# Memory denominators of four head groups as one column-tiled quartet, with the reciprocals moved across partitions by copies

## Chip, cores and metric

One core of one Trainium2 chip. The metric is the device time of one execution in microseconds (us); lower is better. Kernels of one set of rounds ran in turn on the same chip; the sets of the experiments ran on three different chips, so across sets a kernel is best compared by its distance from the kernel before of its own set. An execution counts as fast when it is within 1.5% of the fastest of the same kernel. All times below are of fast executions unless it is said otherwise.

## The reference, cut to what matters

A transformer block: layer norm, an attention with a compressive memory over four segments of 512 tokens (32 heads of 32), output projection, then a gated feed-forward part. The change touches the memory's part of the attention:

```python
for s in range(N):                                   # N = 4 segments
    ...
    pq = phi(qs)
    num = jnp.einsum('bhld,bhde->bhle', pq, M)
    den = jnp.einsum('bhld,bhd->bhl', pq, z)[..., None] + 1e-06   # the memory denominator
    a_mem = num / den
    o = g * a_mem + (1.0 - g) * a_dot                # a_dot: softmax attention, with its own denominator
    ...
    M = M + jnp.einsum('bhld,bhle->bhde', pk, vs)
    z = z + jnp.einsum('bhld->bhd', pk)
```

In the first segment the kernel has no memory part, so the memory denominator is needed in three segments. A segment is worked on in two halves of four groups with four heads each: six half-segments with a memory.

## The kernel before, the parts that matter

Every operation is first recorded in a graph with a cost in ns. A planner then plays the graph through (a list scheduler with priorities), and the order in which each engine gets its instructions is fixed by that play. `SHIFT` is a table of small changes to the priorities, one entry per unit of work, found by a search for the shortest play. On the chip each engine has its list and waits on semaphores.

```python
def schedule(self):                       # the planner
    for o in ops:
        late, cls = SHIFT.get(o.unit, (0, 0))
        o.seq += late + 1e-6 * o.seq
        o.cls += cls
    ...
                    cost = o.cost[e]      # the planned duration decides what comes next
    ...
                    elif e == "dve" and o.port:
                        begin = max(begin, until["pool"])   # port=True: not planned to begin beside a GpSimd instruction
    ...

def finish(self, s, g0, at):              # one half-segment; g0: first of its four groups
    gd = self.queue(4)                    # PSUM bank 4: all denominators
    if s:                                 # memory denominators: 4 full matmuls, 128 columns of weights each
        self.mms(gd, [(lambda gr: self.bank(gr), self.zsel[:, g0 + i, :], self.pq[:, i, :],
                       i == 0, i == 3, 512) for i in range(4)], 2)
    ...
    column(gd, range(4), lambda i, kc, j: self.ones32[:, i, :], ...)   # softmax denominators, tiled 128*32
    ...                                   # column(...) for v: the numerators
    G.op("dve", ..., e.transpose(T1, self.bank(gr)))        # 32x32 blocks: tokens to partitions
    if s:
        ... tensor_scalar(td, td, 1e-6, None, op0=ALU.add)  # on the memory part
    ... reciprocal(rc, tr)                # both kinds at once, into Rc[p, group, kind, block]
    for n, i in enumerate(order):         # per group
        ...
        sp = ... transpose(dst, src)      # Rc back to R, spread over 32 partitions
        ...
        m = self.mms(gm, [(lambda gr: self.bank(gr), Mb, pq, True, True, 512)], 3)   # num
        G.dep(m, sp)                      # planned behind the transpose
        prev = ... scalar_tensor_tensor(R1, self.bank(gr), gcol, R1, ...)   # num * g / den
        ... tensor_tensor(oT, R0, R1, op=ALU.add)
```

The weights zsel of the full matmuls had their columns placed so that the memory denominator of group i, head j came out in partition strip j (32 partitions), next to the softmax denominator of the same head.

The softmax here doesn't subtract the row's maximum and nothing guards it: scores larger than these inputs give would overflow.

## Time and profile before

| | before |
|---|---|
| time, median of 6 executions | 904.32 us (903.87 to 904.83) |
| profiled span | 901.8 us |
| TensorE busy | 896.5 us, 99% |
| matmul engine's own waits | 2.5 us, all before 11 us |
| VectorE, ScalarE, GpSimd busy | 47%, 32%, 20% |

How to read it: the kernel is bound by TensorE's stream of matmuls, and the stream has no holes after the start. The prediction shows the lines. One more view, VectorE's timeline behind one denominator block (start us, length us, engine, line, operation):

```profile
128.25 0.72 DVE L1101 STREAM_TRANSPOSE T<-ps 128x512 f32<-128x512 f32 x1 [1.73 <-PE ps L1080]
...
130.27 0.94 DVE L1114 RECIPROCAL Rc<-T 128x128 f32<-128x128 f32 x1
131.13 0.36 DVE L982 TENSOR_TENSOR Macc<-Macc,ps 128x258 f32<-128x258 f32 x1
131.41 1.23 DVE L1134 STREAM_TRANSPOSE R<-Rc 128x1024 f32<-128x1024 f32 x1
```

The chain is: transpose T1, reciprocal, transposes into R. From the start of T to the first R are 3.16 us.

### The profile page before, as it was taken

The page shows a single profiled execution, that of the slowest core. Times are in us where ns is not written, and L with a number is a line of the kernel's source. Part 1 is how long each engine was busy: PE and PEld are TensorE (multiplying, and loading weights), DVE is VectorE, ACT ScalarE, POOL GpSimd, SP SyncE. Part 2 cuts the span into 40 slices and gives each one's busy share as a digit, 9 for nine tenths or more (in the row PEclk, how much of TensorE's full clock was granted, in tenths as well). Part 3 has the DMA queues.
Part 4 walks back from the last instruction along what each step waited for, and adds up shares of the span by engine and source line. Part 5 has one row for each costly group of instructions (what it writes and reads, how often), then busy time and mean ns, then how long its engine had stood idle before and what let it go on. Part 6 is the DMA issues. An engine that isn't in the chain of part 4 may idle for free.

```text
span 901.8 us, 13023 instructions
## 1 busy us (share of the span) xinstructions
PE 896.5 (99%) x5561; PEld 408.8 (45%) x5561; DVE 423.8 (47%) x653; ACT 286.0 (32%) x306; POOL 179.9 (20%) x243
## 2 busy tenths in 40 slices
PE   8999999999999999999999999999999999999998
PEld 5444444444434444444444444444444444444445
DVE  5683868878685766564434311201343334431111
ACT  6775867686675711111211100000111111110000
POOL 2554546467473422010000000000000000000000
PEclk9999999999999999999999999999999999999999
DMA  7879672545641268554322301013123221301110
GB/s 234 215 203 276 186 151 83 153 140 118 165 117 48 71 234 222 153 155 112 94 74 67 94 30 41 24 47 94 48 76 93 71 66 52 94 24 41 37 40 30
DMA packets 146473, 96.27 MB, mean 107 GB/s; under 512 B 45424, under 2 KB 133616, under 8 KB 146416
## 3 DMA queue, kind: packets, MB, share of 16 engines
q1 hardware_dynamic: 146416, 95.45, 38.5%
q8 instruction: 44, 0.72, 0.3%
q14 instruction: 13, 0.11, 0.0%
HBM read 76.55 MB, written 8.39 MB: 94 GB/s over the span
## 4 chain that ended last, share of the span: by engine, by line
PE 99%; DMA 1%; DVE 0%; SPq 0%; issue 0%
PE ps L701 92%; PE ps L1080 4%; PE ps L1035 3%; DMA xs<-in_A_x_dram 1%; PE ps L713 0%; SPq L292 0%; DVE lnst L827 0%; DVE xnT L725 0%; DVE ob L1229 0%; DVE xs L858 0%; DVE lnve L853 0%
## 5 line engine op out<-in xcount | busy, mean ns | idle before, releaser
L701 PE MATMUL ps<-hnT,w1b 128*128 128x512 bf16 x896 | 220.0, 379 | 0.0
L701 PE MATMUL ps<-hnT,w3b 128*128 128x512 bf16 x896 | 219.1, 379 | 0.0
L1197 ACT ACTIVATE sg<-ps 128x512 bf16<-128x512 f32 x112 | 66.9, 597 | 428.8 <-PE ps L701 428.8
L701 PE MATMUL ps<-w2b,hm 128*128 128x512 bf16 (+1 forms) x924 | 196.4, 373 | 0.0
L1200 DVE SCALAR_TENSOR_TENSOR t<-sg,ps 128x512 bf16<-128x512 bf16 x112 | 76.8, 686 | 192.2 <-ACT sg L1197 192.1
L1047 ACT ACTIVATE et<-ps 128x2048 bf16<-128x2048 f32 x80 | 149.9, 1874 | 29.1 <-PE ps L1035 28.8
L701 PEld LDWEIGHTS ps<-w2b,hm 128*128 128x128 bf16 x924 | 90.4, 98 | 103.3
L701 PEld LDWEIGHTS ps<-hnT,w1b 128*128 128x128 bf16 x896 | 87.1, 98 | 105.9 <-issue 7.6
L701 PEld LDWEIGHTS ps<-hnT,w3b 128*128 128x128 bf16 x896 | 87.2, 98 | 105.6 <-issue 1.0
L1056 POOL TENSOR_SCALAR_AFFINE_SELECT et<-et 128x512 bf16<-128x512 bf16 x96 | 85.3, 895 | 86.8 <-ACT et L1047 79.7
L1205 DVE SCALAR_TENSOR_TENSOR hm<-t,ps 128x512 bf16<-128x512 bf16 x112 | 76.8, 686 | 38.2 <-PE ps L701 35.5
L1229 DVE TENSOR_TENSOR ob<-hr,ps 128x512 bf16<-128x512 bf16 (+1 forms) x33 | 22.2, 671 | 143.0 <-PE ps L701 143.0
L701 PE MATMUL ps<-xnT,wp 128*128 128x512 bf16 (+1 forms) x352 | 62.1, 321 | 0.3 <-DVE lnve L853 0.2
L701 PE MATMUL ps<-wo,oT 128*128 128x512 bf16 x256 | 61.7, 379 | 0.0
L701 PE MATMUL ps<-hnT,wp 128*128 128x512 bf16 x256 | 61.5, 380 | 0.0
L701 PEld LDWEIGHTS ps<-xnT,wp 128*128 128x128 bf16 x352 | 27.6, 98 | 25.3 <-issue 3.5
L701 PEld LDWEIGHTS ps<-wo,oT 128*128 128x128 bf16 x256 | 24.4, 98 | 29.9 <-issue 1.7
L701 PEld LDWEIGHTS ps<-hnT,wp 128*128 128x128 bf16 x256 | 23.2, 98 | 28.7 <-issue 4.1
L1134 DVE STREAM_TRANSPOSE R<-Rc 128x1024 f32<-128x1024 f32 (+1 forms) x32 | 34.5, 1094 | 0.0
L1035 PE MATMUL ps<-qT,kT 32*128 32x128 bf16 (+3 forms) x512 | 31.7, 301 | 0.0
L701 PE MATMUL ps<-wp,hnT 128*128 128x512 bf16 x128 | 31.3, 380 | 0.0
L701 PE MATMUL ps<-wp,xnT 128*128 128x512 bf16 x128 | 31.0, 380 | 0.0
(85 smaller groups left out, 547.3 us busy)
## 6 DMA issues: line engine op xcount, KB each, us to landing
w3b<-in_B_w_dram SPq DMA_DIRECT2D x28, 512.0 KB, 3.9
w1b<-in_B_w_dram SPq DMA_DIRECT2D x28, 512.0 KB, 4.0
wp<-in_A_wv_dram SPq DMA_DIRECT2D x8, 1024.0 KB, 5.5
wp<-in_A_wq_dram SPq DMA_DIRECT2D x7, 1024.0 KB, 5.9
wp<-in_A_wk_dram SPq DMA_DIRECT2D x7, 1024.0 KB, 6.0
w2b<-in_B_w_dram SPq DMA_DIRECT2D x7, 1024.0 KB, 5.6
xs<-in_A_x_dram SPq DMA_DIRECT2D x16, 256.0 KB, 5.3
h<-in_A_x_dram SPq DMA_DIRECT2D x16, 256.0 KB, 3.3
```

Source lines behind the costliest of these rows:

```text
L701: return [e.matmul(p[0](gr), p[1], p[2], start=p[3], stop=p[4]) for p in part]
L1035: ins.append(e.matmul(self.bank(gr, j, 512 - 128 * kc, off), k[r, g0 + g, 128 * kc:128 * kc + 128], q[r, g0 + g, 128 * kc:512], start=True ...
L1047: return [e.activation(et[:, :, :], src, AF.Exp, scale=self.scale)]
L1056: self.pool_op(lambda e, v=v, pat=pat: e.affine_select(v, v, pattern=pat, compare_op=ALU.is_ge, fill=0.0, base=0, channel_multiplier=-1), ...
L1080: ins.append(e.matmul(self.ps[32 * j:32 * j + 32, b * 512 + 128 * kc:(b + 1) * 512], lhsT(i, kc, j), at[i, kc][:, j, :], start=kc == 0 and ...
L1134: sp = self.dve_op(lambda e, dst=dst, src=src: e.transpose(dst, src), dve_ns(512 * nr), [Rc[:, i, 0:nr, :]], [rs], 2)
L1197: self.g.op("act", act_ns(512), lambda e, gr, sg=sg: [e.activation(sg, self.bank(gr), AF.Tanh, scale=0.5)], writes=[sg], cls=0, group=gg)
L1200: e.scalar_tensor_tensor(t1, sg, 1.0, self.bank(gr), op0=ALU.add, op1=ALU.mult)], reads=[sg], writes=[t1], cls=0,
L1205: e.scalar_tensor_tensor(dst, t1, 0.5, self.bank(gr), op0=ALU.mult, op1=ALU.mult)], reads=[t1], writes=[dst], cls=0,
L1229: self.g.op("dve", dve_ns(n), lambda e, gr, hs=hs, ob=ob, n=n: [e.tensor_tensor(ob, hs, self.bank(gr, 0, n), op=ALU.add)], reads=[hs], wri ...
```

## The change

Intent: the four full matmuls use 128 columns of weights where 4 would do. As four column tiles (32 columns each, group i in partition strip i) they should run at once, for the price of one (217 ns by the spacing of the full matmuls before), as the quartets of the ones matmuls do in the trace before (136 ns for one of 320 columns in the mean, which is 320/512 of 217), and inside the operation that already runs tiled. The price: the denominator of group i, head j now comes out in strip i, and belongs in strip j. So the memory reciprocals go to a new tile Rm, and 16 small copies per half-segment carry them from strip to strip. The diff, without the table `SHIFT`, which is new in every entry:

```diff
@@ -605,7 +603,7 @@
         self.ocol = buf("ocol", [128, 8], F32)
         self.mhalf = buf("mhalf", [128, 1], F32)
         self.Mbf = buf("Mbf", [128, 8, 128], BF16)
-        self.zsel = buf("zsel", [128, 8, 128], BF16)
+        self.zsel = buf("zsel", [128, 8, 32], BF16)
         self.Macc = buf("Macc", [128, 8, 129], F32)
         self.lnst = buf("lnst", [128, 32, 12], F32)
         self.lnmv = buf("lnmv", [128, 32, 2], F32)
@@ -637,6 +635,7 @@
         r7 = at[0]
         self.et = [buf(f"et{i}", [128, 4, 512], BF16) for i in range(10)]
         self.Rc = buf("Rc", [128, 4, 2, 16], F32)
+        self.Rm = buf("Rm", [128, 4, 16], F32)
         self.R = [buf(f"R{i}", [128, 2, 512], F32) for i in range(2)]
 
         self.T1 = buf("T1", [128, 512], F32, self.g.base[self.R[1].name][1])
@@ -773,13 +772,13 @@
         o = self.ones32[:, :, :]
         P(lambda e: e.memset(o, 0.0), 128, [], [o], 1)
         for a in range(4):
-            oa = self.ones32[:, a, 2 * a:2 * a + 1]
+            oa = self.ones32[:, a, a:a + 1]
             P(lambda e, oa=oa: e.memset(oa, 1.0), 1, [], [oa], 1)
         for v in self.v:
             vo = v[:, :, :, 128:129]
             P(lambda e, vo=vo: e.memset(vo, 1.0), 32, [], [vo], 2)
         zz = self.zsel[:, :, :]
-        P(lambda e: e.memset(zz, 0.0), 1024, [], [zz], 3)
+        P(lambda e: e.memset(zz, 0.0), 256, [], [zz], 3)
         self.g.dma(self.beta[:, :], bass.AP(self.A_beta.tensor, self.A_beta.offset,
                                             [[0, 128], [1, 32]]), cls=3)
         gc, oc = self.gcol[:, :], self.ocol[:, :]
@@ -989,9 +988,7 @@
         self.either(lambda e, Mb=Mb, am=am, bl=bl: e.tensor_tensor(Mb, am, bl, op=ALU.mult),
                     256, 2, [am, self.blk[:, :]], [Mb], 4)
         for a in range(2):
-            col = 2 * (2 * pr % 4 + a) + 1
-            zs = self.zsel[:, 2 * pr + a, :].rearrange(
-                "p (j n) -> p j n", j=4)[:, :, col:col + 1].rearrange("p j n -> p (j n)")
+            zs = self.zsel[:, 2 * pr + a, 4:8]
             z = self.Macc[:, 2 * pr + a, 128:129]
             hm = self.hmask[:, :]
             self.pool_op(lambda e, zs=zs, z=z, hm=hm: e.tensor_scalar(
@@ -1060,20 +1057,23 @@
     def finish(self, s, g0, at):
 
 
+
         G = self.g
         G.stage()
         v = self.v[s % 2]
         gd = self.queue(4)
-        if s:
-            self.mms(gd, [(lambda gr: self.bank(gr), self.zsel[:, g0 + i, :], self.pq[:, i, :],
-                           i == 0, i == 3, 512) for i in range(4)], 2)
-
-        def column(gr, groups, lhsT, first, reads):
+
+        def column(gr, groups, lhsT, first, reads, zsel=None):
             G.stage()
 
             def emit(e, gr):
                 ins = []
                 b = gr.banks[0]
+                for i in range(4) if zsel else ():
+                    ins.append(e.matmul(
+                        self.ps[32 * i:32 * i + 32, b * 512:(b + 1) * 512],
+                        self.zsel[:, g0 + i, :], self.pq[:, i, :], start=True, stop=True,
+                        tile_position=(0, 32 * i), skip_group_check=True))
                 for i in groups:
                     for kc in range(4):
                         for j in range(4):
@@ -1084,12 +1084,14 @@
                                 tile_position=(0, 32 * j), skip_group_check=True))
                 return ins
 
-            o = self.mark = G.op("pe", len(groups) * (1280 / 2.4 + 12.0), emit,
-                     reads=[at[i, kc] for i in groups for kc in range(4)] + reads, cls=1, group=gr)
+            cost = len(groups) * (1280 / 2.4 + 12.0) + (216.0 if zsel else 0.0)
+            reads = (zsel or []) + [at[i, kc] for i in groups for kc in range(4)] + reads
+            o = self.mark = G.op("pe", cost, emit, reads=reads, cls=1, group=gr)
             o.mode = "col"
 
         column(gd, range(4), lambda i, kc, j: self.ones32[:, i, :], None if s else 0,
-               [self.ones32[:, :, :]])
+               [self.ones32[:, :, :]],
+               [self.zsel[:, g0:g0 + 4, :], self.pq[:, :, :]] if s else None)
         gn = {}
         order = (3, 0, 1, 2)
         for n, i in enumerate(order):
@@ -1101,17 +1103,20 @@
         G.op("dve", dve_ns(512), lambda e, gr: [e.transpose(T1, self.bank(gr))], writes=[T1],
              cls=0, group=gd)
         t1v = self.T1[:, :].rearrange("p (b r) -> p b r", r=32)
-        step = 1 if s else 2
         if s:
-            td = t1v[:, :, 1:8:2]
+            td = t1v[:, :, 4:8]
             self.dve_op(lambda e: e.tensor_scalar(td, td, 1e-6, None, op0=ALU.add), 217.0,
                         [td], [td], 0, port=True)
-            tr = t1v[:, :, 0:8]
-            rc = Rc[:, :, :, :].rearrange("p g t b -> p b (g t)")
-        else:
-            tr = t1v[:, :, 0:8:2]
-            rc = Rc[:, :, 0, :].rearrange("p g b -> p b g")
-        self.dve_op(lambda e: e.reciprocal(rc, tr), 150 + 6.2 * 128 / step, [tr], [rc], 0)
+        Rm = self.Rm
+        for n in range(2 if s else 1):
+            tr = t1v[:, :, 4 * n:4 * n + 4]
+            rc = Rm[:, :, :].rearrange("p j b -> p b j") if n else Rc[:, :, 0, :].rearrange(
+                "p g b -> p b g")
+            self.dve_op(lambda e, tr=tr, rc=rc: e.reciprocal(rc, tr), 150 + 6.2 * 64, [tr], [rc], 0)
+        for i in range(4 if s else 0):
+            for j in range(4):
+                a, b = Rc[32 * j:32 * j + 32, i, 1, :], Rm[32 * i:32 * i + 32, j, :]
+                self.dve_op(lambda e, a=a, b=b: e.tensor_copy(a, b), 90.0, [b], [a], 1)
         prev = None
         for n, i in enumerate(order):
             G.stage()
```

## The prediction

> **What bounds the kernel now.** I read the page's busy shares first, then its chain that ended last, then the table of waits for TensorE, then the timeline around the denominators, then the groups of instructions with shapes kept apart.
>
> ```profile
> PE 896.5 (99%) x5561; PEld 408.8 (45%) x5561; DVE 423.8 (47%) x653; ACT 286.0 (32%) x306; POOL 179.9 (20%) x243
> PE 99%; DMA 1%; DVE 0%; SPq 0%; issue 0%
> ```
>
> TensorE is busy for 896.5 of 901.8 us and 99% of the chain is matmuls. That busy time is a union of overlapping 379 ns records, so it could hide an array that is poorly fed. I therefore checked the waits of the matmul engine itself:
>
> ```profile
> PE ps L701 <- DVE oT L766: 1.2, 1, 1.2
> PE ps L713 <- DVE xs L858: 1.1, 2, 0.7
> PE ps L701 <- DVE lnve L853: 0.2, 1, 0.2
> ```
>
> These three lines are the whole answer, 2.5 us, and all lie in the first 11 us (warm-up and first layer norm). The weight-load row has a longer list, but its largest entries are "issue", in pieces of at most 0.5 us around changes of shape. So nothing that another engine does in the attention stages makes TensorE wait today. A change is worth what it takes out of TensorE's stream, provided it creates no wait that lasts.
>
> The stream around one half-segment's denominators (columns: start us, us, line, operation; x is the number of matmuls):
>
> ```profile
> 106.48 1.04 PE L701 MATMUL ps<-hnT,wp 128*128 128x512 bf16 x4
> 107.35 1.03 PE L701 MATMUL ps<-pq,zsel 128*128 128x512 bf16 x4
> 108.22 1.03 PE L701 MATMUL ps<-hnT,wp 128*128 128x512 bf16 x4
> ...
> 123.79 1.03 PE L701 MATMUL ps<-wo,oT 128*128 128x512 bf16 x4
> 124.75 1.27 PE L1080 MATMUL ps<-et,v 128*32 128x512 bf16 x32
> 125.85 2.35 PE L1080 MATMUL ps<-et,ones 128*32 128x512 bf16 x64
> 128.02 1.26 PE L1080 MATMUL ps<-et,v 128*32 128x512 bf16 x32
> 129.21 0.63 PE L701 MATMUL ps<-v,pkn 128*128 128x129 bf16 x8
> ```
>
> Starts matter here, not the printed lengths[...]. The four memory-denominator matmuls (moving pq, stationary zsel) occupy 108.22 - 107.35 = 0.87 us, or 217 ns each: full-array matmuls in a packed stream. The 64 column-tiled matmuls with the ones weights occupy 128.02 - 125.85 = 2.17 us. They are 16 quartets with widths 512, 384, 256 and 128, mean 320 columns, so a quartet costs 136 ns. If the four of a quartet ran one after another, 64 times 320/512 of 217 ns would be 8.7 us. Four column tiles therefore do run together, at the price of one matmul of their width. In all eight half-segments the column-tiled operations sit in one unbroken block of 128.
>
> [...] The quartets here reach about 4x (136 ns where a single 320-wide matmul would need 320/512 of 217 = 136 ns)[...]. [...] Here: the last full group starts at 123.79 and needs 0.87 us, to 124.66; the block starts at 124.75, so entry costs some 0.09 us. That price is already paid once per block. [...] TENSOR_SCALAR takes 149 ns for 128x1, 155 to 161 ns for 128x8 and 191 ns for 128x64.
>
> **The change, part by part.**
>
> TensorE, removed: 4 full matmuls per half-segment where there is a memory (segments 1 to 3, two halves each, so 6 times; the groups confirm 24 in all):
>
> ```profile
> L701 PE MATMUL ps<-pq,zsel 128*128 128x512 bf16 x24 | 6.2, 380 | 0.0
> L1080 PE MATMUL ps<-et,ones 128*32 128x512 bf16 x128 | 12.5, 379 | 0.0
> L1107 DVE TENSOR_SCALAR T<-T 128x64 f32<-128x64 f32 x6 | 1.1, 191 | 0.1
> L1114 DVE RECIPROCAL Rc<-T 128x128 f32<-128x128 f32 x6 | 5.7, 948 | 0.0
> L1114 DVE RECIPROCAL Rc<-T 128x64 f32<-128x64 f32 x2 | 1.1, 538 | 0.0
> ```
>
> TensorE, added: one quartet of 512 columns, emitted in the same operation as the ones matmuls, in the same tile shape (128*32). So no extra mode change, and by the quartet arithmetic it costs one matmul, 217 ns. Matmul and weight-load counts stay the same. Saving: 4 x 217 - 217 = 651 ns per half-segment, 6 x 651 ns = 3.9 us, all on the path that sets the end. If loading four 32-column weights ahead of the quartet exposed one weight load (97 ns in this trace), it would be 0.6 us less; the ones block shows no such gap, since its quartets already take what their columns need.
>
> VectorE: the reciprocal of 128x128 (948 ns) becomes two of 128x64 (538 each): +128 ns. The addition of 1e-6 stays 64 elements wide: 0. New: 16 copies of 32x16 f32 that move memory reciprocals from group i's partition strip to head j's. None is in the trace. A MEMSET takes 59 ns (32x1) and 85 ns (32x32), which puts 16 elements near 72 ns; the TENSOR_SCALAR times above, which read SBUF as the copies do, put 16 elements near 163 ns. I take 115 ns as an estimate between, so 1.8 us for 16 and about 2.0 us per half-segment with the reciprocals, 12 us over six. VectorE goes from 424 to about 436 us (431.5 to 440 with the two ends). These copies lie after the reciprocal and before the four block transposes into R, so the memory part of each half-segment (R, the Mbf matmul, oT) comes some 2 us later. That is off TensorE's path as long as TensorE has other work queued. It has: in the 13 us after the block at 124.75 it alternates hnT,wp, wo,oT and Mbf matmuls without a wait.
>
> GpSimd: clearing zsel falls from 1024 to 256 elements (1030 ns once, at 1.8 us). TensorE waits there for VectorE and input loads. Worth 0.
>
> Placement: the long table of shifts is new throughout, so all engines' orders are re-tuned. I can size only the room it has. TensorE waits just 2.5 us, all at the start, and the count of mode changes is fixed by 80 score operations plus 8 blocks unless two happen to touch. So it can hardly gain more than 1 us and can lose that or more.
>
> Sum: 904.4 - 3.9 + about 0.4 for imperfect refilling and small losses = 900.9 us.
>
> **The rivals.** (1) The lengthened VectorE chain becomes a wait. For it: VectorE is busy 44.1, 48.8 and 40.3 of 60 us in the stretches from 100 to 160, 160 to 220 and 220 to 280 us, up to 81%, and it also empties the three PSUM banks that feed the dense matmuls. Against: it would only rise by some four points there, the copies are short so an eviction waits for one of them rather than 2 us, and no PSUM wait exists now. If all 2.0 us showed six times, the net is -3.9 + 12 = +8, or 912 us. If one time in six, 902.5. (2) The quartet doesn't overlap, because four different moving operands (one per group) are read at once. Against: the ones and v quartets also have four different moving operands, one per head. This would give 904 to 905 us. (3) The time saved before 322 us is lost in the feed-forward tail, because weights arrive no sooner. For: from 322 us on TensorE runs without pause (577.2 us busy of 579). Against: DMA engines are only 28% busy there, and just one wait for such a load, 0.4 us, is in the weight-load waits. This would give 903 to 904 us. (4) Re-tuning changes the start-up or the number of mode changes: 1 us either way.
>
> **Range and chances.** The main term is a count times a measured spacing, on the engine that bounds the kernel, so I put the middle at 900.9. Gains below 900.4 need luck in rival 4, so the low end is close, 899.5; losses from rivals 1 and 3 are more plausible, so the high end is 903.2. Two per cent is 18 us: a win of that size would need over four times what is removed; a loss of that size would need more than twice the full VectorE chain exposed. Hence 0.01 faster, 0.98 same, 0.01 slower.
>
> **What would show it right or wrong.** Right: the 24 pq,zsel matmuls appear as 128*32 inside the column block, which grows from 4.46 to about 4.68 us with no second block; the matmul engine's own waits stay near 2.5 us; the uninterrupted tail begins about 3.5 us earlier than 322. VectorE gains 96 copies of 32x16, with mean between 70 and 165 ns, and 12 reciprocals of 128x64. Wrong: the block grows by 0.5 us or more (quartet not concurrent); matmul waits on R, oT or PSUM evictions appear after 40 us (VectorE exposed); the tail starts earlier but contains new DMA waits (rival 3).

The sum: 904.4 - 3.9 + about 0.4 = 900.9 us, with the 3.9 from 6 x (4 x 217 - 217) ns of the trace before and the 0.4 an allowance of mine. That the quartet runs as one matmul rests on the measured 136 ns alone. As to printed lengths and starts: the four matmuls print 1.03 us, and the next group starts after 0.87.

## The result, and the profile after

The changed kernel took 906.84 us (median of 6, 905.56 to 907.45) against 904.32 us: 2.5 us slower, where 3.4 us less had been predicted. The ratio is 1.0025, 95% interval 1.0012 to 1.0038. Ratios here are the mean time of one kernel's fast runs over that of the other's fast runs of the same rounds, so not quite the ratio of the medians quoted. By the 2% rule this is "same"; the measured time lies outside the predicted range, on the other side of the kernel before.

From the page of the changed kernel, busy shares and the chain that ended last (it was 99% TensorE before):

```profile
PE 895.0 (99%) x5561; PEld 406.3 (45%) x5561; DVE 439.2 (49%) x755; ACT 286.5 (32%) x306; POOL 173.5 (19%) x243
PE 91%; DVE 5%; DMA 2%; issue 1%; SPq 0%; DVEq 0%
```

Busy shares hardly move; the chain shows that VectorE is now on the path for 5%, some 45 us. The quartet itself did what was predicted (TensorE's timeline; starts matter):

```profile
126.58 1.27 PE L1080 MATMUL ps<-et,v 128*32 128x512 bf16 x32
127.67 0.39 PE L1073 MATMUL ps<-pq,zsel 128*32 128x512 bf16 x4
127.89 2.35 PE L1080 MATMUL ps<-et,ones 128*32 128x512 bf16 x64
```

Four matmuls in 127.89 - 127.67 = 0.22 us, as against 0.87 before. Then TensorE runs on, and meets this:

```profile
137.31 1.90 PE L700 MATMUL ps<-wo,oT 128*128 128x512 bf16 x8
140.15 0.38 PE L700 MATMUL ps<-pq,Mbf 128*128 128x512 bf16 x1 [0.94 <-DVE R L1139]
```

Eight full matmuls from 137.31 need 1.73 us, to 139.04; the next starts at 140.15. So 1.1 us passed in which nothing was fed (the bracket says 0.94, as it counts from the modelled end of the last record). The matmul waits for R. It takes no data from R: the wait is the one that the kernel adds itself, `G.dep(m, sp)` in the code above. R waits for this, in VectorE's timeline of the same kernel:

```profile
132.94 0.54 DVE L1115 RECIPROCAL Rm<-T 128x64 f32<-128x64 f32 x1
...
133.76 2.71 DVE L1119 COPY Rc<-Rm 32x16 f32<-32x16 f32 x14
136.50 0.69 DVE L724 CAST qT<-ps 128x512 bf16<-128x512 f32 x1
137.23 0.37 DVE L1119 COPY Rc<-Rm 32x16 f32<-32x16 f32 x2
137.63 2.37 DVE L1139 STREAM_TRANSPOSE R<-Rc 128x1024 f32<-128x1024 f32 x2
```

Here the transpose T starts at 130.29, so from T to the first transpose into R it is 7.3 us, where it was 3.2 us before. Fourteen copies in a row take 2.71 us, 194 ns each, and sixteen in one piece elsewhere 3.20 us. All 96 by the line's own view (min/median/max ns): 

```profile
L1119 DVE COPY Rc<-Rm x96: 149/166/568, 133.8 to 347.2; 32x16 f32<-32x16 f32 x96
```

A record of 166 ns and some 31 ns before the next one starts: **about 197 ns from start to start, where the plan has 90**. The matmul engine's own waits, which were 2.5 us before:

```profile
PE ps L700 <- DVE R L1139: 1.6, 2, 0.9
...
PE ps L700 <- DVE qT L724: 0.8, 1, 0.8
PE ps L700 <- DVE t L1205: 0.6, 2, 0.4
PE ps L700 <- DMA pkn<-pk: 0.6, 1, 0.6
PE ps L700 <- DVE R L1153: 0.3, 1, 0.3
PE ps L700 <- DVE hm L1210: 0.3, 1, 0.3
```

Waits for R, but also for PSUM evictions (qT, t, hm) that stand behind the copies on VectorE.

**An account of TensorE's stream.** The view of waits understates, since a record's modelled end hides up to 160 ns (a full matmul of 512 columns has a record of 379 ns and starts 216 ns before the next). I therefore took the start of every matmul (of every quartet for tiled ones) in the trace and split the distance to the next start into three parts: what an undisturbed neighbour needs (0.417 ns a column + 2.7 ns, a line through the spacings in these traces, 216 ns at 512 columns and 56 ns at 128), what is usual at a change of tile shape (0.10 us in the mean of the 176 in the kernel before; counted up to 0.135), and the rest, called stall. From 12 us on, in us:

| run | stream | changes of shape | stall | profiled span |
|---|---|---|---|---|
| before | 868.26 | 17.62 (176 changes) | 1.01 | 901.80 |
| changed | 864.93 | 18.16 (180 changes) | 6.86 | 904.87 |
| difference | -3.33 | +0.54 | +5.85 | +3.07 |

The three differences add up to 3.06 of the 3.07 us. The stream is 3.33 shorter and not 18 x 0.216 = 3.89, because the start was later: 10 more of the 128-column matmuls (56 ns each, 0.56 us) lie behind the 12 us mark. The four extra changes of shape come from two column blocks that the new order splits in two. So the question is what made 5.85 us of stalls.

### The profile page after: what moved, and what is told of

It is laid out like the page before. It is cut to its first block, busy times and chain, and to the rows that moved or that the text cites. A ratio compares the mean times of both kernels' runs of the same rounds, so it can differ in the third digit from the quotient of the medians.

```text
span 904.9 us, 13112 instructions
## 1 busy us (share of the span) xinstructions
PE 895.0 (99%) x5561; PEld 406.3 (45%) x5561; DVE 439.2 (49%) x755; ACT 286.5 (32%) x306; POOL 173.5 (19%) x243
## 4 chain that ended last, share of the span: by engine, by line
PE 91%; DVE 5%; DMA 2%; issue 1%; SPq 0%; DVEq 0%
PE ps L700 85%; PE ps L1080 3%; PE ps L1032 2%; DVE Rc L1119 2%; DVE R L1139 1%; DMA wp<-in_A_wq_dram 1%; DMA xs<-in_A_x_dram 1%; DMA pkn<-pk 1%; DVE T L1103 0%; DVE qT L724 0%; DVE Nsb L1130 0%; DVE Rm L1115 0%; DVE t L1205 0%; DVE Rc L1115 0%; DVE hn L841 0%
## 5 line engine op out<-in xcount | busy, mean ns | idle before, releaser
L700 PE MATMUL ps<-hnT,w1b 128*128 128x512 bf16 x896 | 222.3, 379 | 0.3 <-DVE t L1205 0.3
L1144 POOL TENSOR_TENSOR R<-Nsb,R 128x512 f32<-128x512 f32 x20 | 26.1, 1319 | 35.8 <-DVE R L1139 35.8
```

The source lines that it names most:

```text
L700: return [e.matmul(p[0](gr), p[1], p[2], start=p[3], stop=p[4]) for p in part]
L1144: self.either(lambda e, o1=o1, Ns=Ns, R0=R0: e.tensor_tensor(o1, Ns, R0, op=ALU.mult), 512, 2, [Ns, R0], [o1], 2)
```

## The experiments

Theory A: the copies take 197 ns where the planner counted 90. In the fixed order of TensorE, the matmuls that wait for R, or for an eviction behind the copies, stand where they would have been ready with 90 ns. Rival B: the new table is a worse order in itself (split blocks, waits for transfers), whatever the copies take. Rival C: the quartet costs more than it seems. Rival D, later: VectorE with the copies is too loaded for any order.

Two aids were used for the expectations: the planner's own play, which gives 903.65 us for the kernel before and 900.45 for the changed one (it expected the same gain as I did), and a replay of its fixed orders with other durations. The replay of the changed kernel's order gives:

```
copy planned at 90 ns, played at   90     120     150     197 ns
time                             900.4   902.5   905.4   909.9 us
```

It is too pessimistic at 197 (measured 906.8), but its stalls lie where the trace has them. These are calculations and not runs; the runs follow. All used five rounds.

### 1. No copies, same order

The planner sees the copies; at emission they are left out. The orders of TensorE, ScalarE and the DMA queue came out identical to those of the changed kernel.

```diff
+            if o.skip:                     # a copy: emit nothing, hand on the reciprocal's token
+                last = max((d for d in o.deps if d.eng == e), key=lambda d: d.tok[1])
+                o.tok, o.snap = last.tok, last.snap
+                continue
...
+        # once, at the start: e.memset(Rc[:, :, 1, :], 1.0)
```

> The changed kernel with every engine's order kept, the 96 copies left out and the memory reciprocals' slots filled with ones (wrong result on purpose). Theory A (the copies take 197 ns each from start to start where the kernel's planner counted 90, so the matmuls that need them stand too early in TensorE's fixed order): the stalls after 130 us shrink from 6 us to under 1 us and the time is 900.9 us, within 1 us, which is the prediction's sum. Rival B (the new table of shifts is itself worse: two more mode changes, waits for weights and for the transposed pk): 905 to 907 us, as the order is the same. Rival C (the column-tiled quartet costs more than a matmul): also 905 to 907.

Measured: 900.65 us (899.94 to 901.07), ratio to before 0.9961 (0.9948 to 0.9973). The column-tiled quartet, the new table, the split blocks and the two reciprocals are all still there. VectorE's timeline and the matmul that stalled before:

```profile
133.27 0.55 DVE L1123 RECIPROCAL Rm<-T 128x64 f32<-128x64 f32 x1
...
136.30 2.36 DVE L1148 STREAM_TRANSPOSE R<-Rc 128x1024 f32<-128x1024 f32 x2
```

```profile
137.64 1.90 PE L706 MATMUL ps<-wo,oT 128*128 128x512 bf16 x8
139.38 0.38 PE L706 MATMUL ps<-pq,Mbf 128*128 128x512 bf16 x1
```

The matmul on Mbf now starts 1.74 us after the eight before it, without a wait. Account: stream 865.16, changes 18.04, stall 1.03 us. B and C fall, but for the half microsecond of shape changes: the same order without the copies gives the predicted 900.9 to within 0.3 us.

### 2. Half of the copies, same order

```diff
+                o.skip = i >= 2            # copies of groups 0 and 1 only
```

> The same with the copies of two groups of four kept, 8 per half-segment (wrong result for the other two groups). Theory A: 8 copies at 197 ns are 1.58 us, close to the 1.44 us that the planner had set aside for 16, so nearly nothing is exposed: 901.2 us, within 1. If VectorE's load as such mattered (each copy costs the same wherever it lies), the time would be half way between the run without copies and the changed kernel, 903.9. Rival B: 905 to 907.

Measured: 901.44 us (900.38 to 902.05), stall 1.65 us. Eight copies cost 0.8 us, the next eight 5.4 (906.84 - 901.44; the two were timed in different sets of rounds, whose kernel before differs by 0.3). The cost is not per copy: it begins where the real duration passes the planned one, 8 x 197 = 1.58 against 16 x 90 = 1.44 us.

### 3. Useless copies in the kernel before

The other direction: own table, own order, but copies that the planner doesn't know of, behind each reciprocal.

```diff
+            for k in range(8 if s else 0):         # the second run: 16
+                i, j = divmod(k, 4)
+                last = e.tensor_copy(self.Rm[32 * j:32 * j + 32, i, :],
+                                     self.T1[32 * i:32 * i + 32, 0:16])
```

> The kernel before with its own table and order, and 8 useless copies of 32x16 behind each of its six reciprocals with memory, which the planner does not know of (1.6 us each time, about what the changed kernel's copies take beyond their plan). Theory A: the stalls appear here too, at the matmuls on Mbf: about 5 us more, 909 us (907 to 912). Rival B (the copies are harmless, the changed table is to blame): 904 to 905.5.

> The same with 16 copies, 3.15 us behind each reciprocal, none of it planned. Theory A: exposed almost in full beyond any slack, about 10 us more than the kernel before, 915 us (911 to 921). Rival B: 904 to 906.

Measured: 907.46 us with 8 (906.27 to 908.91), 915.99 us with 16 (915.04 to 916.12; 4 executions), against 904.01. Stalls 3.84 and 12.59 us. Theory A holds from this side too, and rival B again falls: a table that had no stalls gets them from the copies alone. The first eight cost 3.4 us and the second eight 8.5, which would fit some slack that the first used up (not shown). Three of the four executions with 16 copies show a granted clock of 0.998; the one at 1.0 took 915.04 us. The copies were shorter here than the expectations counted: emitted as one operation, they follow one another every 179 ns and not 197, 1.35 us for 8 and 2.79 us for 16. With 16, the matmul engine waits, besides for the start, for evictions behind the copies (three of nine lines):

```profile
PE ps L702 <- DVE Macc L983: 3.1, 2, 1.7
PE ps L702 <- DVE qT L726: 2.5, 2, 2.1
PE ps L702 <- DVE t L1209: 1.8, 2, 1.5
```

### 4. The copies planned at their true duration, and two controls

The table fits one set of costs only: with the copies at 200 ns and the delivered table, the planner's play takes 953 us. So each of the following has a table of its own, from a search of mine (random changes kept when the planner's play got shorter, 14 minutes, from an empty table, the same for each).

```diff
-                self.dve_op(lambda e, a=a, b=b: e.tensor_copy(a, b), 90.0, [b], [a], 1)
+                self.dve_op(lambda e, a=a, b=b: e.tensor_copy(a, b), 200.0, [b], [a], 1)
```

> The changed kernel, complete and correct, with one number changed, the planner's cost of a copy from 90 to 200 ns, and the table of shifts searched anew for it (the old table does not fit once a cost changes). The planner itself says 899.8 us. Theory A: with the true duration planned, TensorE's fixed order puts other matmuls ahead of those that need the reciprocals, and the stalls go: 900.5 us, 899.5 to 902, although VectorE still does all 96 copies. Rival D (the copies load VectorE so much that no order hides them): 903 or more.

The second control keeps 90.0 and changes the table only:

> The second control: the changed kernel with the copies planned at 90 ns as delivered, and a table from the same search. Planner: 899.9 us, as good as with true costs. Theory A: the plan is broken on the chip in the same way, stalls at the matmuls on Mbf, 906 us (904 to 908.5). If it comes out at 901, the delivered table was merely unlucky and the cost of the copies doesn't matter.

The first control is the kernel before with a new table:

> Control for the search: the kernel before with a table from the same search (same time, same start). Planner: 903.5 us against 903.65 with its own table. Expected 904 us, within 1 of the kernel before; if it comes out near 901, the gain of the run with true costs belongs to the search and not to the cost.

And one with the copies on either engine:

```diff
+                G.op(("act", "dve"), {"act": 210.0, "dve": 200.0}, move, reads=[b], writes=[a], cls=1)
```

> The same, but each copy may go to ScalarE (planned at 210 ns) or VectorE (200 ns), whichever the planner finds free; own table, correct result. Planner: 899.7 us. Theory A: TensorE bounds the kernel and the copies are hidden already, so shortening their chain gains nothing: within 0.7 us of the run with true costs. If VectorE were still a bound (rival D), this one would be over 1 us faster than that run.

| run | median us (range) | ratio to before (95%) | stall us |
|---|---|---|---|
| copies at 200 ns | 902.86 (901.42 to 903.58) | 0.9986 (0.9972 to 0.9999) | 3.67 |
| copies at 90 ns, new table | 907.93 (906.51 to 908.29) | 1.0042 (1.0029 to 1.0054) | 8.38 |
| before, new table | 904.18 (903.98 to 904.26) | 1.0005 (0.9992 to 1.0017) | 1.46 |
| copies on two engines | 902.89 (902.34 to 905.05) | 0.9997 (0.9984 to 1.0009) | 3.58 |
| before, same rounds | 903.68 (903.15 to 904.49) | | |

The two controls come out as theory A has it: the search gives the kernel before nothing, and two unrelated tables with the copies at 90 ns, the delivered one and this, have 5.9 and 7.4 us more stalls than the kernel before. One number in the plan, 90 to 200, is worth 5.1 us between kernels that the planner thinks equal. But the run with true costs missed its expectation of 900.5 by 2.4 us, and rival D was not ruled out by it: 3.67 us of stalls were left, of which 1.7 us were two waits for transfers and 1.2 us two waits for VectorE. Two engines for the copies gained nothing over one, as expected.

Where do the stalls for VectorE come from with the duration planned? The trace of the two-engine run had a hint (timeline, two engines):

```profile
175.18 1.27 POOL L1143 TENSOR_TENSOR R<-Nsb,R 128x512 f32<-128x512 f32 x1 [1.39 <-DVE R L1138]
175.44 2.09 DVE L1115 COPY Rc<-Rm 32x16 f32<-32x16 f32 x2
176.40 1.10 POOL L1045 TENSOR_SCALAR_AFFINE_SELECT et<-et 128x1024 bf16<-128x1024 bf16 x1
```

Two copies in 2.09 us: the first lasted from 175.44 to 176.48, until the GpSimd instruction ended at 176.45, and the second about as long as the next one. In the runs seen so far every copy over 250 ns (2 in the changed kernel, of 278 and 568 ns, 6 with true costs, 9 with two engines, 5 in the control at 90 ns) had started while a GpSimd instruction ran and ended within about 30 ns of its end (22 and 21 ns after it in the changed kernel). This is called the lock below; what causes it no run shows. The planner has a rule for such pairs, under the name `port`, but it was not set for these copies. Such copies do reach TensorE: in the run with true costs the chain behind the larger of its two waits for VectorE, 0.95 us at 299.57, holds two of them (772 and 1043 ns).

### 5. The lock planned too

```diff
-                self.dve_op(lambda e, a=a, b=b: e.tensor_copy(a, b), 200.0, [b], [a], 1)
+                self.dve_op(lambda e, a=a, b=b: e.tensor_copy(a, b), 200.0, [b], [a], 1,
+                            port=True)
...
-    DMA_RATE = 260.0                      # first two runs only: later landings
-    DMA_FIX = 1900.0
+    DMA_RATE = 240.0
+    DMA_FIX = 2400.0
```

> The complete, correct change with the copies planned at 200 ns, with a lock against GpSimd (every copy over 250 ns in the earlier runs had started while a GpSimd instruction ran and ended just after it), and with later landings of transfers in the plan (the run with true costs waited for weights three times, 2.2 us). Table searched anew; planner 901.2 us, of which the later landings cost about 1 us at the start that the chip does not have. Theory A with these two corrections: no stall over 0.3 us after 12 us but small ones, 900.5 us (899.5 to 902), so about 3.5 us under the kernel before. If the rest of the run with true costs comes from something else, 902 to 903.5 again.

> The same plan with another table (another seed of the search, same planner's span of 901.2 us), to see how far tables of equal plan differ on the chip: within 1 us of the first, 900.5.

The control without the lock, with a second table:

> The plan with true costs but without lock and later landings, with another table (another seed, planner 899.9 us): 902.5 us (901 to 904), as the first of this kind; over 1 us slower than the two with the lock planned if that correction is real.

And, to tell the two corrections apart, the lock alone:

> Which of the two corrections carries the last 3 us: the copies planned at 200 ns and with the lock against GpSimd, but with the planner's old, earlier landings of transfers. Table searched anew, planner 899.9 us. If the lock carries it: 900 to 901 us with no wait for VectorE over 0.3 us, and at most waits for transfers. If the later landings carry it (they make the plan looser everywhere near a load): 902 to 903.5, with stalls as in the two runs with true costs alone.

| run | median us (range) | ratio to before (95%) | stall us |
|---|---|---|---|
| lock and later landings | 900.03 (see below) | 0.9952 (0.9938 to 0.9965) | not profiled fast |
| the same, second table | 899.74 (899.67 to 900.66) | 0.9953 (0.994 to 0.9967) | 0.89 |
| true costs, second table | 902.95 (902.18 to 903.01) | 0.9983 (0.997 to 0.9995) | 3.55 |
| before, same rounds | 904.38 (903.86 to 905.87) | | |
| lock alone | 900.86 (899.89 to 903.68) | 0.9969 (0.9956 to 0.9982) | see below |
| before, its rounds | 903.98 (903.52 to 905.96) | | |

These kernels compute the right result, do all 96 copies, and the better one beats the kernel before by 4.6 us (899.74 against 904.38) and the changed one, across sets of rounds, by 7 us. Rival D is out: VectorE is busy 433.8 us in the best of them and nothing waits for it. From that kernel's page, and all waits of its matmul engine, all at the start:

```profile
PE 892.8 (99%) x5561; PEld 407.3 (45%) x5561; DVE 433.8 (48%) x745; ACT 287.9 (32%) x309; POOL 183.8 (20%) x250
```

```profile
PE ps L693 <- DVE oT L758: 1.2, 1, 1.2
PE ps L705 <- DVE xs L850: 0.9, 1, 0.9
PE ps L693 <- DVE lnve L845: 0.3, 1, 0.3
```

What the plan does differently is seen behind one block of this kernel: sixteen copies from 129.96 to 133.56 (3.60 us, one of them held by GpSimd for 0.6), transposes into R at 136.04, and the first matmul on Mbf at 139.55, 1.1 us after the transposes end at 138.40. In the changed kernel it was due at 139.04, while its transpose ended only at about 140.

The lock alone gave 900.86 us, with a wider range. Its trace, in which about 90 matmul records are missing, so that the account can't be made, shows a wait of 0.8 us for a load of h and none over 0.2 us for VectorE after the start. Its slowest execution, 903.68 us, is the only one at a granted clock of 0.998; the others took 899.89 to 901.59.

How much is the lock's? By medians against the kernel before of the same rounds, the two kernels with true costs are 0.8 and 1.4 us faster, lock alone 3.1, lock and later landings 4.4 and 4.6. So of the last 3.4 us some 2 go to the lock and 1.4 to the landings. This split is not clear of the noise: the intervals of the lock alone and of its neighbours overlap, it had one table, and the later landings were not run without the lock.

That the lock matters is better seen in the traces. In the second table with true costs, three waits for VectorE make 2.5 of the 3.55 us of stalls (0.96, 0.81 and 0.75 us), and each has a copy held for about 1 us in the chain before it (1076, 962 and 1017 ns). In the lock-alone run seven copies are still held, the longest 1211 ns, and nothing waits for them: planning the lock does not remove it, but makes the plan long enough. From the first to the last copy of a half-segment, its play has 7.3 and 9.6 us in the two longest cases, and the chip took 7.2 and 9.2; without the lock the play has 3.9, 5.7 and 5.9 us before those three stalls, and the chip took 5.4, 7.3 and 7.6.

One execution of the first of these runs took 1886.97 us, the other four 899.88 to 900.09. The profile fell on that one: around 700 us full matmuls of 512 columns follow one another at 472 ns in the mean (443 is the median of the whole execution, 216 is usual), and the mean record in each of the six largest groups of 512-column matmuls is 664 to 679 ns, where 379 is usual, all at a recorded clock of 1.0. The commonest instructions of the other engines took no longer than usual (in the mean 688 and 687 ns for t and hm on VectorE, 686 in the kernel before; 597 ns for sg on ScalarE in both). It is left out of the ratio. I cannot say what it was; it happened in none of the other executions.

## Why the prediction was wrong

- **The bound and the saving were right.** TensorE bounds the kernel, the quartet runs at the price of one matmul (0.22 us, worked out 0.217), inside the tiled block, and with the copies out of the way the total is 900.65 us where the sum had 900.9.
- **The step that failed: "These copies lie after the reciprocal and before the four block transposes into R, so the memory part of each half-segment (R, the Mbf matmul, oT) comes some 2 us later. That is off TensorE's path as long as TensorE has other work queued."** It had other work, but behind the waiting matmul. Nothing behind it on TensorE's list went ahead of it (1.1 us empty before 140.15, the next matmuls from 140.36); "queued" is no help unless the planner put it ahead. I read the absence of waits before as slack. It only showed that plan and chip agreed. What the runs showed in its place: the 16 copies take 3.2 us where the plan has 1.44, and in that fixed order they made 5.85 us of new stalls, which were gone when the copies were left out (1.03 us left, 1.01 before). There was little room: in the kernel before, 1.35 us of unplanned copies behind each of six reciprocals already cost 3.4 us, and 2.79 us cost 12.
- **What should have been compared stood in the diff:** 90.0 ns a copy, 1.44 us in the plan. My own estimate was 115 ns, 1.84 us, already beyond it; the replay makes that 902.5 us at 120. I used the estimate to load VectorE and never against the plan.
- **The mis-sized term:** a copy takes 197 ns from start to start, so 3.2 us per half-segment and 19 us in all, for 1.8 and 11. Averaging a MEMSET with a TENSOR_SCALAR was the error; the row of the instruction that reads SBUF (163 ns at 16 elements, by the TENSOR_SCALAR rows) was within 2% of the record (166), and I had left out the 31 ns between two. The prediction's own test "mean between 70 and 165 ns" failed at 173. One sum was off as well: a loss of 2% needs 18 + 3.9 = 22 us of exposed waits, 1.8 times the 12 us of the chain and not "more than twice".
- **Rival 1 was the right one and got the wrong weight.** Its reason against, that an eviction waits for one copy only, does not hold in a fixed order: evictions and transposes stand behind all the copies that the list puts before them (qT, t and hm in the waits). Around 174 us sixteen copies with one eviction between them and two transposes ran before the eviction of qT at 180.49, for which the matmul at 181.12 had waited 0.8 us.
- **Rival 2 (no overlap) and rival 3 (saving lost in the tail) did not occur.** Rival 4 (re-tuning) is worth 0.54 us of changes of shape and perhaps part of the 0.56 us at the start; the sizes held, the sign was against.
- **The signs named ahead:** the column block grew from 4.46 to 4.68 us as predicted, but only in four of six half-segments; the other two are split. The last column-tiled matmul starts at 341.61 us, not 3.5 us earlier than the 321.84 of the kernel before. That sign says little: without the copies it is still at 336.51, and the total is as predicted.
- The plan needed more than one correction: the duration (about 5 us), the lock with GpSimd (about 2 us) and the later landings (about 1.4 us; the split of these two is rough). Whether the loss also goes when the Mbf matmuls no longer wait for R (`G.dep`) was not run.

## What to carry to other kernels

In a kernel whose engine orders are fixed ahead, "no waits in the profile" means that plan and chip agree, not that there is slack: compare the duration of every new instruction with the cost that the plan gives it, before anything else. A small instruction costs its record plus the gap to the next (here 166 + 31 ns for 16 elements), and here sixteen times over; and if some of its records last until a GpSimd instruction ends (here up to 1211 ns for the usual 166), plan that too. When a change with a sound gain comes out slower, run it with the suspected part left out and the orders held: one run then separated the gain (3.4 us) from the loss.

## What else the traces show

- In the changed kernel, copies that follow one another never overlap: 31 ns in the median (29 to 32) lie between the end of one and the start of the next, and a semaphore increment follows each copy. In experiment 3, where it follows the last copy only, the gap is 13 ns. No run shows that the increment is the reason.
- A short GpSimd instruction need not hold the copies. In the changed kernel eight copies that started inside a recorded TENSOR_SCALAR of 128x4 on GpSimd took 164 to 241 ns, and two of them ended 46 and 96 ns before it did; the two held for longer (278 and 568 ns) had started inside a select over 512 elements.
- The account has 17.6 us for the 176 changes of tile shape in the kernel before, 0.10 us each. The quartets here reach 4x (0.22 us for four matmuls of 512 columns that took 0.87).
- For the one execution of 1886.97 us, in which full matmuls of 512 columns start every 443 ns in the median at a recorded clock of 1.0, whether TensorE ran at a reduced clock that the record misses is not shown.
